# Attention and two MLPs: the first streamed pair's g @ w_out by seven products, first weight slices kept in SBUF, late x, q, k and v in slots

## The chip, the core and the metric

The kernel runs on one core of a Trainium2 chip. The metric is device time in microseconds (us) of one execution. TensorE (PE) multiplies, VectorE (DVE) and ScalarE (ACT) do elementwise work, SyncE (SP) issues the DMA transfers in the order of its queue. Each engine takes its instructions in a fixed order that is settled when the program is built.

## What is computed

Three parts follow each other: a causal linear attention with decay (4 sequences of 768, 8 heads of 64), an MLP with the gate h * sigmoid(1.702 h), and an MLP with the gate max(h, 0) + alpha * min(h, 0). All is fp32.

```python
for t in range(S):
    state = gamma * state + einsum('bhd,bhe->bhde', k[:, :, t], v[:, :, t])
    y[:, :, t] = scale * einsum('bhd,bhde->bhe', q[:, :, t], state)
x = y as 3072 tokens x 512
h = x @ w_in;  g = h * (1 / (1 + exp(-1.702 * h)));  x = g @ w_out      # 512 x 2048, 2048 x 512
h = x @ w_in2; g = maximum(h, 0) + alpha * minimum(h, 0);  out = g @ w_out2
```

## The kernel before

**Precision.** A product of fp32 operands is made of three fp32r matmuls: each operand is split into hi (a rounded copy, made by ACT) and lo (the rest, by a DVE subtraction), and hi*hi, lo*hi and hi*lo are added in PSUM. `g_split`, `x_split`, `piece_hi` and `piece_lo` make such splits. A matmul here has a 128x128 stationary part and 512 moving columns.

**Tokens and blocks.** 24 attention chunks of 128 tokens (`att_scores`, `att_out`, `att_x`, numbered c) make the x of 6 blocks j of 512 tokens. The first MLP's blocks 0 and 1 are multiplied in the plain way, one of 16 slices (ft) of the hidden width at a time: `mlp_h` (12 matmuls) and `mlp_y` (12 matmuls, L558). These are the 32 `steps`. The other work is streamed in five `PAIRS` (layer, pair of blocks): (1,1), (1,2), (2,0), (2,1), (2,2), called 0 to 4 here.

**Pairs by seven products.** A pair's x @ w_in goes through a Strassen-like scheme of 7 products of half blocks in place of 8. For each `quad` (two slices of the hidden width) there are 7 units; `h_unit` (L650) issues 6 matmuls for a unit (L662) and takes one piece of w_in (hi and lo of 256 columns in one slot of 2 KB a partition, `hw`) from DRAM, loaded HRING = 6 units ahead by `load_h`. The pieces are a11, a12, a22 and the combinations s1 to s4, which DVE makes from the raw slices (`conv_sums`, L272, 4 operations for a quad) and `conv_split` (L294) splits and stores to DRAM (`wc`). The pair's g @ w_out runs YLAG = 36 units behind. In pairs 1 to 4 it goes by seven products too (`y_split` L692 makes combinations of g and their splits, `strassen_y` L743 issues 6 matmuls at L760, `y_out` L772 adds the products up). In pair 0 it is plain: `y_chunk` calls `mlp_y` with w_out slices that `load_wo` (L638) brings back from DRAM into a ring of 6 (`woh`, `wol`), 12 matmuls for each of 16 slices and 2 blocks. While it runs, `slice_sums` (L287) adds hi and lo of the same slices up again, from which the combined w_out pieces of pair 1 are made.

**Conversion.** The weights come as 8-byte words and are converted on the chip (`conv_words`, `conv_f32`, L176 to L199), the first layer's beside the plain steps, the second layer's beside pairs 0 and 1 (`W2_AT` gives their slots). In the first layer hi and lo are whole tiles of 512 columns (`whi` L224, `wlo` L242), kept until they are stored and their last plain step is done (`drop`).

**Slots.** Nearly everything in SBUF lives in 82 slots of 2 KB a partition: `take` takes the slot that has been free longest, `give` puts one back; a slot that a store is reading comes back late (`give_stored`, `let_go`). Counting takes and gives through the program, the fewest free slots are 8 at job slot 42, 9 at 76, 4 at 92 and 93, and 4 at 108 and 109.

**Order.** `jobs` is a table by job slot: two job slots for each of the 32 plain steps, so base = 64, then two for 7 units. q, k and v of chunks 4 to 23 and the weights are loaded through `ld`, a ring of 5 tiles, in the order in which the jobs use them (`issue`, L143); the next load is issued when the oldest tile is done. `load_early` (L163) loads chunks 1 to 3 into slots. x of chunks 8 to 15 (pair 0) is written to DRAM by `att_x` (L425) and read back by `x_load`; x of chunks 16 to 23 stays in slots (`att_x_kept`, L434). A scheduler then orders the recorded instructions on each engine, by priority and by when their inputs are there.

Of the kernel before, what the change touches and what calls it, by code (L numbers as in the profile page):

```python
# [8 lines left out]
F32 = mybir.dt.float32  # L9
# [9 lines left out]
P = 128  # L19
# [48 lines left out]
W2_AT = [3 + 1.17 * m for m in range(12)] + [18 + 2 * m for m in range(4)] + [26 + 1.2 * m for m in range(16)]  # L68
# [3 lines left out]
def tile_linear_attention_two_mlps(ctx: ExitStack, tc, qk, kv, w1, w2, consts, alpha, out):  # L72
# [101 lines left out]
    w_hi, w_lo, conv, raw = {}, {}, {}, {}  # L174
# [76 lines left out]
    def put_two(dst, at, part_, src):  # L251
        c = slice(256 * part_, 256 * part_ + 256)
        put(dst[at:at + 2, :, c].rearrange("g p c -> p g c"), src.rearrange("p (g c) -> p g c", g=2))

    def store(key):
        kind, layer, ft = key
        hi, lo = w_hi[key], w_lo[key]
        dst, at = wc[kind, layer, ft // 2], W_AT[kind]
        if kind == "out":
            put(wo[ft][0], hi)  # L260
            put(wo[ft][1], lo)
        elif ft % 2 == 0:
            put_two(dst, at["a11"], 0, hi)
            put_two(dst, at["a11"], 1, lo)
        else:
            put(dst[at["a22"], :, 0:256], hi[:, 256:])
            put(dst[at["a22"], :, 256:512], lo[:, 256:])
        stored.add(key)
# [17 lines left out]

    def slice_sums(i):  # L287
# [4 lines left out]
        conv_sums("out", 1, i)  # L292

    def conv_split(kind, layer, i):  # L294
        for name, s in zip(("s1", "s3"), sums.pop((kind, layer, i))):
# [5 lines left out]
            give_stored(*ws)  # L301
# [101 lines left out]
    def att_x(c):  # L403
        if c >= 4 * BT // C:
            att_x_kept(c)
            return
# [9 lines left out]
        if j < 2:  # L416
            if i == 0:
                new_x(j)
            nc.scalar.copy(out=x_hi[j][:, :, cols], in_=x32)  # L419
            if early_x:  # L420
                att_state(c)
            att[c] = x32
            return
        idx = j // 2 - 1
        for d in range(2):  # L425
            nc.sync.dma_start(
                out=xsd[idx][:, :, d, j % 2, cols].rearrange("k p c -> p k c"), in_=x32[:, 2 * d:2 * d + 2, :]
            )
        att.pop(c)
        give(x32)  # L430
        if c % (2 * BT // C) == 2 * BT // C - 1:
            stored.add(("x", idx))
# [113 lines left out]
    def mlp_y(layer, j, ft, begin, end, carry, w, es=range(NP)):  # L546
        if begin and es[0] == 0:
# [3 lines left out]
        wh, wl = w  # L551
        cols = lambda w, e: w[:, e * P:(e + 1) * P]
        prods = [(e, cols(w, e), gh) for e in es for w in (wh, wl)]
        prods += [(e, cols(wh, e), gl) for e in es]
        seen = [0] * NP
        for e, w, g in prods:
# [490 lines left out]
```

## Time and profile before

| | |
|---|---|
| time, median of 3 runs | 1060.81 us (1060.52 to 1062.38) |
| the profiled execution | 1061.71 us, its span 1059.9 us |
| TensorE busy | 1038.3 us (98%) |
| DVE busy | 849.8 us (80%) |
| ACT busy | 655.2 us (62%) |
| DMA | 292 MB, 276 GB/s over the span |

The span is the time from the first to the last instruction; the execution's own time has some 1.8 us more around it. A busy time is the union of the intervals in which an engine had an instruction at work. The profile also tells which event ended each idle time, the busy time by stretches of the span, and the chain of waits that ended last.

### The profile page before, as it was taken

Reading aid. Unit: us, or ns where it says so; the run is one execution under the profiler, and the core shown is the slowest. Engines: PE = TensorE matmul, PEld = TensorE weight load, DVE = VectorE, ACT = ScalarE, POOL = GpSimd, SP = SyncE. Lnnn points to the kernel's source line nnn. Section 1 sums busy time; section 2 is a strip of 40 time slices with the busy share of each in tenths; the row PEclk is TensorE's granted clock in tenths of the full one; section 3 lists DMA queues with packets and bytes.
Section 4 is the critical chain, followed back from the end, with each engine's and each line's share of the span. In section 5 each row is a group of like instructions: output and inputs, shape, how many; then the busy total and the mean of one; then the engine's idle time right before and its main releaser. Section 6 shows DMA issues by size and latency. Waiting matters only on the chain.

```text
span 1059.9 us, 17734 instructions
## 1 busy us (share of the span) xinstructions
PE 1038.3 (98%) x5980; PEld 848.0 (80%) x5980; DVE 849.8 (80%) x1602; ACT 655.2 (62%) x1344; POOL 0.2 (0%) x4
## 2 busy tenths in 40 slices
PE   8999999999999999999999999999999999999998
PEld 5688887788777888888888878778888888888886
DVE  6999945574568887898899999999786987677792
ACT  7787744454466665556786577777565765556740
POOL 0000000000000000000000000000000000000000
PEclk9999999999999999999999999999999999999999
DMA  8679969789789989999999899888686765675661
GB/s 301 219 257 366 341 232 365 242 290 338 260 304 322 358 299 329 346 332 336 314 306 337 253 323 347 308 275 278 217 270 211 233 221 172 230 253 177 201 199 60
DMA packets 154138, 292.06 MB, mean 276 GB/s; under 512 B 16448, under 2 KB 33216, under 8 KB 154048
## 3 DMA queue, kind: packets, MB, share of 16 engines
q1 hardware_dynamic: 153760, 290.66, 80.8%
q8 instruction: 48, 0.79, 0.3%
q14 instruction: 42, 0.34, 0.1%
q10 hardware_dynamic: 288, 0.27, 0.1%
HBM read 214.32 MB, written 76.55 MB: 274 GB/s over the span
## 4 chain that ended last, share of the span: by engine, by line
PE 78%; DVE 9%; DMA 7%; ACT 3%; issue 2%; SPq 1%; DVEq 0%; ACTq 0%
PE py L760 24%; PE pa L662 16%; PE py L558 16%; PE pd L662 12%; PE ph L537 7%; DMA ld<-kv 2%; DMA wcin<-wb 2%; PE px L361 2%; DVE gl L525 1%; ACT v L326 1%; PE sc L333 1%; DVE gw L517 1%; DMA hw<-wcin 1%; DVE wb L216 1%; DVE gw L677 1%
## 5 line engine op out<-in xcount | busy, mean ns | idle before, releaser
L662 PE MATMUL pa<-xo,hw 128*128 128x512 f32 x960 | 243.6, 390 | 3.8 <-ACT gw L512 2.0
L760 PE MATMUL py<-gh,yw 128*128 128x512 f32 x896 | 240.3, 390 | 1.0 <-DMA yw<-wcout 0.7
L662 PEld LDWEIGHTS pa<-xo,hw 128*128 128x128 f32 x960 | 179.4, 188 | 43.2 <-ACT gw L512 3.0
L760 PEld LDWEIGHTS py<-gh,yw 128*128 128x128 f32 x896 | 167.9, 188 | 37.2 <-DMA yw<-wcout 1.4
L525 DVE TENSOR_TENSOR gl<-gw,gh 128x512 fp32r<-128x512 f32 x224 | 150.2, 688 | 44.6 <-ACT gh L524 38.5
L662 PE MATMUL pd<-xo,hw 128*128 128x512 f32 x720 | 182.7, 390 | 0.0
L524 ACT CAST gh<-gw 128x512 fp32r<-128x512 f32 x224 | 136.2, 620 | 62.6 <-PE py L760 22.5
L662 PEld LDWEIGHTS pd<-xo,hw 128*128 128x128 f32 x720 | 134.8, 188 | 28.3
L760 PE MATMUL py<-gl,yw 128*128 128x512 f32 x448 | 138.3, 390 | 1.8 <-DVE gl L525 1.8
L760 PEld LDWEIGHTS py<-gl,yw 128*128 128x128 f32 x448 | 83.9, 188 | 19.9 <-DVE gl L525 2.6
L517 DVE SCALAR_TENSOR_TENSOR gw<-t,nalpha,gw 128x512 f32<-128x512 f32 x96 | 71.4, 748 | 12.5 <-ACT gw L516 12.3
L515 ACT ACTIVATE t<-gw 128x512 f32<-128x512 f32 x72 | 45.5, 632 | 50.3 <-DVE gw L677 46.3
L773 DVE TENSOR_TENSOR yc<-py,yc 128x512 f32<-128x512 f32 x79 | 50.9, 685 | 26.5 <-PE py L760 26.5
L326 ACT ACTIVATE v<-ld,cst 128x64 f32<-128x64 f32 x168 | 44.4, 336 | 40.1 <-DMA ld<-kv 30.3
L212 ACT CAST wb<-s 128x256 fp32r<-128x256 f32 x128 | 48.0, 404 | 33.6 <-DVE s L279 17.9
L674 ACT COPY gw<-pa 128x512 f32<-128x512 f32 x80 | 46.3, 581 | 25.5 <-PE pa L662 25.1
L677 DVE TENSOR_TENSOR gw<-pd,gw 128x512 f32<-128x512 f32 x80 | 54.9, 686 | 5.0 <-PE pd L662 4.8
L216 DVE TENSOR_TENSOR wb<-s,wb 128x256 fp32r<-128x256 f32 x128 | 50.2, 420 | 8.1 <-ACT wb L212 7.5
L537 PE MATMUL ph<-xhi,whi 128*128 128x512 f32 x128 | 51.4, 402 | 1.5 <-ACT xhi L419 1.1
L558 PE MATMUL py<-gh,whi 128*128 128x512 f32 x128 | 51.2, 400 | 0.5 <-ACT gh L524 0.5
L558 PE MATMUL py<-gh,wlo 128*128 128x512 f32 x128 | 50.1, 392 | 0.0
L537 PE MATMUL ph<-xhi,wlo 128*128 128x512 f32 x128 | 50.1, 391 | 0.0
(100 smaller groups left out, 1608.9 us busy)
## 6 DMA issues: line engine op xcount, KB each, us to landing
hw<-wcin SPq DMA_DIRECT2D x280, 256.0 KB, 4.5
yw<-wcout SPq DMA_DIRECT2D x200, 256.0 KB, 3.6
ld<-w SPq DMA_DIRECT2D x64, 512.0 KB, 5.3
wcin<-wb SPq DMA_DIRECT2D x88, 256.0 KB, 5.0
wcout<-wb SPq DMA_DIRECT2D x88, 256.0 KB, 3.9
ld<-qk SPq DMA_DIRECT2D x21, 512.0 KB, 5.4
ld<-kv SPq DMA_DIRECT2D x21, 512.0 KB, 5.2
xl<-xsd SPq DMA_DIRECT2D x32, 256.0 KB, 4.8
```

The lines of the kernel that those rows point to most:

```text
L212: nc.scalar.copy(out=w[:, 0:256], in_=src)
L216: nc.vector.tensor_tensor(out=w[:, 256:], in0=src, in1=w[:, 0:256].bitcast(F32), op=ALU.subtract)
L326: nc.scalar.activation(out=v[:, h, :], in_=vt[:, h * D:(h + 1) * D], func=AF.Copy, scale=decay_v[:, h:h + 1])
L517: nc.vector.scalar_tensor_tensor(out=g, in0=t, scalar=nalpha[:, ft:ft + 1], in1=g, op0=ALU.mult, op1=ALU.add)
L524: nc.scalar.copy(out=gh, in_=g)
L525: nc.vector.tensor_tensor(out=gl, in0=g, in1=gh.bitcast(F32), op=ALU.subtract)
L537: nc.tensor.matmul(out=ph, lhsT=w[:, k * P:(k + 1) * P], rhs=x[:, k, :], start=(n == 0), stop=(n == len(prods) - 1),)
L558: nc.tensor.matmul(out=py[e], lhsT=w, rhs=g, start=(begin and seen[e] == 1), stop=(end and seen[e] == 3))
L662: nc.tensor.matmul(out=ps, lhsT=w[:, 256 * part_ + k * P:256 * part_ + (k + 1) * P], rhs=x[2 * k + low], start=(n in (0, 1, 3) and m == 0) ...
L677: nc.vector.tensor_tensor(out=g, in0=ps, in1=g, op=ALU.add)
L760: nc.tensor.matmul(out=ps[e], lhsT=w[:, at:at + P], rhs=t, start=(fresh and seen[e] == 1), stop=(m == GQ - 1 and seen[e] == 3), skip_group ...
L773: add_ = lambda o, x: nc.vector.tensor_tensor(out=o, in0=ps, in1=x, op=ALU.add)
```

## The change

Four edits, and what they need:

1. Pair 0's g @ w_out goes by the seven products as in the other pairs (IDX_S, `ysteps`, `load_wo` and the plain branch of `y_chunk` go). So the combined pieces of the first layer's w_out have to be there before pair 0: `slice_sums` and `conv_split` for it become jobs at slots `SUMS_OUT` (47 to 68). For four quads the slices' hi and lo are still in SBUF then; for the other four (`LOADED`) `slice_load` brings them back, two slots earlier. The quads of pair 0 run in the order 6, 7, 4, 5, 0, 1, 2, 3 (`QORD`), those of pair 1 forward.
2. The first layer's weights are split and stored in halves like the second layer's (`stored_parts`, `conv_hi`, `conv_lo`, `store`): one slot holds hi and lo of 256 columns. For quads 6 and 7 (`RESIDENT`) the seven w_in pieces stay in their slots, and the first 14 units take them from there (`resident`, `load_h`, `drop`).
3. x of chunks 8 to 15 stays in slots (`att_x_kept` from chunk 8 on); the write to DRAM and `x_load` of pair 0 go.
4. q, k and v of chunks 16 to 23 are loaded by `load_early` at job slots base + (-5, -3, -1, 1, 2, 3, 4, 5), where their scores stand at base + 0 to 7, instead of through the ring `ld`.

`W2_AT` is changed slightly. The number of slots stays 82; the fewest free ones are now 4 at job slot 42, 3 at 76, 4 at 92 and 93, 6 and 7 at 108 and 109.

```diff
-IDX_S = 1
-QORD = [tuple(range(8)) if i != 1 else tuple(range(7, -1, -1)) for i in range(5)]
-WSTEPS = 6
+QORD = [(6, 7, 4, 5, 0, 1, 2, 3)] + [tuple(range(8))] * 4
+SUMS_OUT = (62, 64, 66, 68, 47, 51, 55, 58)
+LOADED = 4
+RESIDENT = (6, 7)
+LOADS = (-5, -3, -1, 1, 2, 3, 4, 5)
-W2_AT = [3 + 1.17 * m for m in range(12)] + [18 + 2 * m for m in range(4)] + [26 + 1.2 * m for m in range(16)]
+W2_AT = [3 + 1.17 * m for m in range(12)] + [17 + 1.5 * m for m in range(6)] + [26 + 1.25 * m for m in range(14)]
...
     def conv_hi(key):
+        parts = halves(conv[key][0])
+        ms = stored_parts(key) if key[1] == 2 else (0, 1)
+        w_of[key] = {m: piece_hi(parts[m]) for m in ms}
+
+    def conv_lo(key):
+        t = conv.pop(key)[0]
+        for m, w in w_of[key].items():
+            piece_lo(w, halves(t)[m])
...
-        hi = w_hi[key]
-        w_lo[key] = take("wlo", dtype=F32R)
-        nc.vector.tensor_tensor(out=w_lo[key], in0=t, in1=hi.bitcast(F32), op=ALU.subtract)
...
+    def slice_load(i):
+        for f in (2 * i, 2 * i + 1):
+            assert ("out", 1, f) in stored
+            kept[f] = take("wo", dtype=F32R), take("wo", dtype=F32R)
+            for n in range(2):
+                nc.sync.dma_start(out=kept[f][n].bitcast(F32), in_=wo[f][n])
+
     def slice_sums(i):
         for f in (2 * i, 2 * i + 1):
+            ws = kept.pop(f, None)
             raw["out", 1, f] = t = take("wsum")
-            hi, lo = wring[f]
-            nc.vector.tensor_tensor(out=t, in0=hi.bitcast(F32), in1=lo.bitcast(F32), op=ALU.add)
+            for m, part_ in enumerate(halves(t)):
+                hi, lo = halves((ws or w_of["out", 1, f])[m].bitcast(F32))
+                nc.vector.tensor_tensor(out=part_, in0=hi, in1=lo, op=ALU.add)
...
             give(s)
-            give_stored(*ws)
+            if (kind, layer) == ("in", 1) and i in RESIDENT:
+                for m, w in zip(("s1", "s2") if name == "s1" else ("s3", "s4"), ws):
+                    resident[i, m] = w
+            else:
+                give_stored(*ws)
...
     def att_x(c):
-        if c >= 4 * BT // C:
+        if c >= 2 * BT // C:
             att_x_kept(c)
             return
...
             quad, n = units[u]
+            if (quad, W_OF[n]) in resident:
+                hw.append(resident.pop((quad, W_OF[n])))
+                return
             load_piece(hw, "hw", "in", PAIRS[quad // NQ][0], quad % NQ, n)
...
-        if ychunks[c][0] == "o":
-            _, n, half = ychunks[c]
-            idx, t, f = ysteps[n]
...
-            mlp_y(1, 2 * PAIRS[idx][1] + t, f, first, end, None, wring[f], range(2 * half, 2 * half + 2))
...
-        job(s_scores, att_scores, c, load=(("qk", c), ("kv", c)))
+        if c < 4 * per:
+            job(s_scores, att_scores, c, load=(("qk", c), ("kv", c)))
+        else:
+            job(LOADS[c - 4 * per] + base, load_early, c)
+            job(s_scores, att_scores, c)
...
+    for i in range(NQ):
+        if i < LOADED:
+            job(SUMS_OUT[i] - 2, slice_load, i)
+        job(SUMS_OUT[i], slice_sums, i)
+        job(SUMS_OUT[i] + 1, conv_split, "out", 1, i)
```

Three places in the order of the built programs. On TensorE, where pair 0's g @ w_out begins (`pa` is an accumulator of a unit, `py` one of g @ w_out, `gh` and `gl` the split g), before:

```order
L662 MATMUL pa<-xo,hw 128x512 x6
L558 MATMUL py_4108<-gh,woh 128x512
L558 MATMUL py_4108<-gh,wol 128x512
L558 MATMUL py_4109<-gh,woh 128x512
L558 MATMUL py_4109<-gh,wol 128x512
L558 MATMUL py_4108<-gl,woh 128x512
L558 MATMUL py_4109<-gl,woh 128x512
L662 MATMUL pa<-xo,hw 128x512 x6
```

and now:

```order
L632 MATMUL pa<-xo,hw 128x512 x12
L632 MATMUL pd<-xo,hw 128x512 x12
L632 MATMUL pa<-xo,hw 128x512 x6
L705 MATMUL py<-gh,yw 128x512 x4
L705 MATMUL py<-gl,yw 128x512 x2
L632 MATMUL pa<-xo,hw 128x512 x6
L705 MATMUL py<-gh,yw 128x512 x4
L705 MATMUL py<-gl,yw 128x512 x2
```

The chunks stand at the same place behind the units, six matmuls each; before there were 64 such chunks in the pair, now 56.

On the DMA queue (SP), beside units 9 to 21, where the late chunks' q, k and v are loaded (`ld` is the ring, `early` a slot, `w` second-layer words, `wcout` the store of combined w_out pieces), before:

```order
L610 DMA hw<-wcin_3_91 128x512
L610 DMA hw<-wcin_2_90 128x512
L151 DMA ld<-w 128x1024
L151 DMA ld<-qk 128x1024
L151 DMA ld<-kv 128x1024
L151 DMA ld<-w 128x1024
L610 DMA hw<-wcin_3_91 128x512
```

and now:

```order
L171 DMA early<-qk 128x512 x2
L171 DMA early<-kv 128x512 x2
L238 DMA wcout_2_106<-wb 128x512 x4
L591 DMA hw<-wcin_4_92 128x512
L591 DMA hw<-wcin_5_93 128x512
L591 DMA hw<-wcin_4_92 128x512
L591 DMA hw<-wcin_5_93 128x512
L171 DMA early<-qk 128x512 x2
L171 DMA early<-kv 128x512 x2
L153 DMA ld<-w 128x1024
```

The loads of q, k and v are out of the ring, and stores of combined w_out pieces stand between them.

On DVE, beside units 37 to 43 of pair 0, with the first chunks of g @ w_out (`cvt` is a weight in conversion, `t` and `gw` on L668 combinations of g), before:

```order
L677 TENSOR_TENSOR gw<-pa,gw 128x512
L525 TENSOR_TENSOR gl<-gw,gh 128x512
L188 TENSOR_SCALAR cvt<-cvt 128x512
L191 TENSOR_SCALAR cvt<-cvt 128x512
L194 ISA cvt<-cvt,cvr 128x1024
L677 TENSOR_TENSOR gw<-pa,gw 128x512
L525 TENSOR_TENSOR gl<-gw,gh 128x512
L195 SCALAR_TENSOR_TENSOR cvt<-ld,cvt 128x512
```

and now:

```order
L190 TENSOR_SCALAR cvt<-cvt 128x512
L193 TENSOR_SCALAR cvt<-cvt 128x512
L196 ISA cvt<-cvt,cvr 128x1024
L668 TENSOR_TENSOR t_4586<-gw 128x512
L197 SCALAR_TENSOR_TENSOR cvt<-ld,cvt 128x512
L668 TENSOR_TENSOR t_4542<-gw 128x512
L668 TENSOR_TENSOR gw<-gw,t_4586 128x512
L668 TENSOR_TENSOR gw<-gw,t_4542 128x512
L514 TENSOR_TENSOR gl<-t_4542,gh 128x512
L514 TENSOR_TENSOR gl<-t_4619,gh 128x512
```

The differences of `y_split` (L668) now stand here too, between the conversion's operations and the splits.

## Rows read from the trace of the kernel before

**Rows 1.** The page: busy us (share of the span) and instructions by engine.

```profile
PE 1038.3 (98%) x5980; PEld 848.0 (80%) x5980; DVE 849.8 (80%) x1602; ACT 655.2 (62%) x1344; POOL 0.2 (0%) x4
```

**Rows 2.** Stretches: from:to, length, busy us by engine (instructions), clock, DMA share, GB/s.

```profile
60.00:140.00 80.00, 80.00 (x384) 66.07 (x378) 71.93 (x140) 59.25 (x115) 0.00 (x0) 1.00 0.94 328
140.00:246.20 106.20, 104.05 (x945) 83.41 (x944) 65.71 (x143) 49.87 (x130) 0.00 (x0) 1.00 0.85 292
246.20:326.40 80.20, 76.50 (x815) 61.93 (x814) 49.30 (x118) 44.37 (x117) 0.00 (x0) 1.00 0.81 287
326.40:489.80 163.40, 162.43 (x715) 133.82 (x714) 135.50 (x280) 96.95 (x203) 0.00 (x0) 1.00 0.96 338
489.80:560.00 70.20, 70.20 (x311) 58.12 (x311) 64.34 (x123) 53.66 (x107) 0.00 (x0) 1.00 0.93 314
560.00:720.00 160.00, 156.26 (x683) 127.21 (x682) 156.02 (x293) 115.46 (x226) 0.00 (x0) 1.00 0.91 308
720.00:1005.60 285.60, 285.60 (x1262) 236.57 (x1261) 223.67 (x353) 177.21 (x312) 0.00 (x0) 1.00 0.70 222
```

**Rows 3.** Timeline of PE at 740 us: start, us, engine, line, operation, count.

```profile
740.27 1.52 PE L662 MATMUL pa<-xo,hw 128*128 128x512 f32 x6
741.63 1.07 PE L760 MATMUL py<-gh,yw 128*128 128x512 f32 x4
742.99 1.52 PE L662 MATMUL pa<-xo,hw 128*128 128x512 f32 x6
```

**Rows 4.** Groups by line and shape: pair 0's plain matmuls, first and last of three.

```profile
L558 PE MATMUL py<-gh,woh 128*128 128x512 f32 x128 | 49.8, 389 | 0.0
...
L558 PE MATMUL py<-gl,woh 128*128 128x512 f32 x128 | 39.4, 389 | 0.0
```

**Rows 5.** Timeline of DVE at 666 us, operations that follow each other without a gap.

```profile
666.13 0.68 DVE L525 TENSOR_TENSOR gl<-gw,gh 128x512 fp32r<-128x512 f32 x1
666.73 0.42 DVE L216 TENSOR_TENSOR wb<-s,wb 128x256 fp32r<-128x256 f32 x1
667.07 0.42 DVE L216 TENSOR_TENSOR wb<-cvt,wb 128x256 fp32r<-128x256 f32 x1
```

**Rows 6.** Groups on DVE: count, busy us and mean ns, idle us before them.

```profile
L242 DVE TENSOR_TENSOR wlo<-cvt,whi 128x512 fp32r<-128x512 f32 x32 | 21.9, 685 | 0.7 <-ACT whi L224 0.7
...
L216 DVE TENSOR_TENSOR wb<-cvt,wb 128x256 fp32r<-128x256 f32 x48 | 19.6, 420 | 2.6 <-ACT wb L212 2.6
...
L291 DVE TENSOR_TENSOR wsum<-woh,wol 128x512 f32<-128x512 f32 x16 | 10.5, 685 | 2.7 <-PE py L558 2.7
...
L442 DVE TENSOR_TENSOR xl<-px,cst 128x128 f32<-128x128 f32 x16 | 4.4, 282 | 0.7 <-PE pu L361 0.7
```

**Rows 7.** Waits of ACT and PE, 246.2 to 326.4 us: us in total, times, longest.

```profile
ACT v L326 <- DMA ld<-kv: 23.2, 6, 5.7
...
PE pa L662 <- ACT gw L512: 2.0, 2, 1.1
```

**Rows 8.** The chain of waits: start, us, what.

```profile
167.18 6.22 DMA wcin<-wb
...
304.16 6.33 DMA ld<-kv
```

**Rows 9.** Waits of PE from 560 to 720 us, the longest.

```profile
PE py L760 <- DVE gl L525: 1.8, 1, 1.8
```

**Rows 10.** DMA: a load to landing; the queue's wait for DVE; the fullest 20 us.

```profile
ld<-kv SPq DMA_DIRECT2D x21, 512.0 KB, 5.2
...
SPq L249 <- DVE wb L216: 56.3, 40, 5.3
...
340.00:360.00 20.00, 20.00 (x89) 16.23 (x88) 16.02 (x31) 13.46 (x27) 0.00 (x0) 1.00 1.05 398
```

More of the change, by code (lines that the diff above doesn't have):

```diff
@@ L255, in store @@
     def store(key):
         kind, layer, ft = key
[L257 to L267, printed above, removed]
+        first = {("in", 0): "a11", ("in", 1): "a22", ("out", 0): "a11", ("out", 1): "a12"}[kind, ft % 2]
@@ L268, in store @@
+        for n, m in enumerate(stored_parts(key)):
+            if (kind, layer) == ("out", 1):
+                dst = wo[ft][m]
+            else:
+                dst = wc[kind, layer, ft // 2][W_AT[kind][first] + n]
+            put(dst, w_of[key][m])
         stored.add(key)
@@ L415, in att_x @@
         cols = slice(i * C, (i + 1) * C)
[L416 to L432, printed above, removed]
+        if i == 0:
+            new_x(j)
+        nc.scalar.copy(out=x_hi[j][:, :, cols], in_=x32)
+        if early_x:
+            att_state(c)
+        att[c] = x32
     def att_x_kept(c):
         banks = att.pop(c)
-        t, i = divmod(c - 4 * BT // C, BT // C)
+        t, i = divmod(c % (2 * BT // C), BT // C)
         for k in range(2):
@@ L544, in mlp_h, with mlp_y @@
             g_of[1, j, ft] = g_split(g)
-    def mlp_y(layer, j, ft, begin, end, carry, w, es=range(NP)):
-        if begin and es[0] == 0:
+    def mlp_y(layer, j, ft, begin, end, carry, w):
+        if begin:
             for e in range(NP):
@@ L550, in mlp_y @@
         gh, gl = g_of[layer, j, ft]
[L551 to L554, printed above, removed]
+        prods = [(e, cols(w, low, e), gh) for e in range(NP) for low in range(2)]
+        prods += [(e, cols(w, 0, e), gl) for e in range(NP)]
         seen = [0] * NP
-        for e, w, g in prods:
+        for e, lhsT, g in prods:
             seen[e] += 1
             nc.tensor.matmul(
-                out=py[e], lhsT=w, rhs=g, start=(begin and seen[e] == 1), stop=(end and seen[e] == 3)
+                out=py[e], lhsT=lhsT, rhs=g, start=(begin and seen[e] == 1), stop=(end and seen[e] == 3)
             )
@@ L926, in drop @@
             if key in stored:
-                give(w_hi.pop(key), w_lo.pop(key))
+                kind, _, ft = key
+                keep = {}
+                if kind == "in" and ft // 2 in RESIDENT:
+                    keep = {m: {0: ("a11", "a12"), 1: ("", "a22")}[ft % 2][m] for m in stored_parts(key)}
+                for m, w in w_of.pop(key).items():
+                    if m in keep:
+                        resident[ft // 2, keep[m]] = w
+                    else:
+                        give(w)
             else:
@@ L931, in finish_step @@
     def finish_step(s, step):
-        w = w_hi["out", 1, step[2]], w_lo["out", 1, step[2]]
-        mlp_y(*step, w)
+        mlp_y(*step, w_of["out", 1, step[2]])
         if uses["out", step[2]] == s:
@@ L947, in tile_linear_attention_two_mlps @@
         let_go(2)
-        if s == NF + LEAD:
-            for u in range(HRING):
-                load_h(u)
-    load_wo(0)
     for s, step in queue:
@@ L954, in tile_linear_attention_two_mlps @@
     drop()
+    for u in range(HRING):
+        load_h(u)
     turn = {"split": 0, "chunk": 0}
@@ L964, in y_turn @@
             turn["chunk"] += 1
-    old = 4 * NF * IDX_S
     for u in range(len(units)):
@@ L969, in tile_linear_attention_two_mlps @@
         past = u + 1 - YLAG
+        if past == -2 * YRING:
+            for c in range(YRING):
+                load_y(c)
         if past > 0:
-            y_turn(min(8 * past // NU, old) + max(0, past - old * NU // 8))
+            y_turn(past)
         if u % NU in (3, 6):
```

133 lines of the change are left out of this document (40 added, 93 removed).

## The prediction, made before the result was known

> **What bounds the kernel now.** I read the page's busy times first: TensorE is busy 1038.3 us of the span of 1059.9, DVE 849.8, ACT 655.2 [rows 1]. 21.6 us are left in which TensorE does nothing, so a change pays here only if it takes matmuls away or takes some of those 21.6 us, and it costs as soon as it adds idle time. Then the stretches [rows 2]; I name them by what runs in them. B (140 to 246.2 us) is the rest of the first two blocks with attention chunks 8 to 15, C (246.2 to 326.4) the first 36 units of g = gate(x @ w_in) with chunks 16 to 23, D (326.4 to 489.8) the first streamed pair's g @ w_out beside units, E (to 560) and F (to 720) the next pair with the second layer's weight conversion, G the rest. The idle time of TensorE (length less busy) is 2.15 in B, 3.70 in C, 0.97 in D, 0 in E, 3.74 in F and 0 in G. DVE is at 92% in E, where TensorE never waits, and at 97.5% in F, where it waits; the wait seen there is one for gl by DVE, 1.8 us [rows 9]. The granted clock is 1.00 in every stretch, the upper level of 2.4 GHz. In the timeline twelve matmuls of 128x512 follow each other in 742.99 - 740.27 = 2.72 us [rows 3]: 0.2267 us each is the price of a matmul on the path.
>
> The profiled execution took 1061.7 us, the median of the runs is 1060.8: I sum against 1061.7 and take 0.9 off at the end.
>
> **TensorE.** In D the old form is three groups of 128 matmuls, 384 in all [rows 4]. The new form has 2 groups of quarters x 7 products x 4 slice pairs x 6 matmuls = 336. 48 fewer, 48 x 0.2267 = 10.9 us, all on the path, since D is TensorE's by 162.43 of 163.40 us. Everything else on TensorE has the same count. The Trainium skill, page "TensorE: Matmul & The Clock Gate", section "Wait — 56ns, not 53.3ns?", gives 215.7 ns from start to start for 512 columns at the upper clock. By that the saving would be 10.4 us; the rows of this kernel say 226.7 ns, and I use them.
>
> **DVE.** Back to back, an operation on 512 columns takes 666.73 - 666.13 = 0.60 us and one on 256 takes 667.07 - 666.73 = 0.34 [rows 5]; the line through both gives an estimate of 0.21 for 128. The change adds:
> - hi and lo of the first layer's weights in halves: 64 x 0.34 for 32 x 0.60 (L242 goes, L216 grows) [rows 6], +2.6 us, nearly all before 140 us.
> - sums of the w_out slices in halves: 32 x 0.34 for 16 x 0.60 (L291) [rows 6], +1.3.
> - x of chunks 8 to 15 written by 32 operations of 128 columns for 16 of 256 (the form is L442) [rows 6]: 6.7 - 5.4 = +1.3, in B.
> - the pair's seven products: 24 more splits, 32 differences, and 20 additions for 4 copies: (24 + 32 + 16) x 0.60 = +43.2 in D.
> Together +48 us. And it moves: the 16 + 32 + 32 operations that make the combined w_out pieces leave D (9.6 + 10.9 + 10.9 = 31.4 us) and go to B and C. Counted in the order between the matmuls that begin and end the stretches, DVE's work grows by 1.8 before B, 22.6 in B, 14.8 in C, 15.7 in D (11.8 by the above, the rest is second-layer conversion that comes earlier) and falls by 7.2 behind D. B then has 65.7 + 22.6 = 88 busy of 106, C 49.3 + 14.8 = 64 of 80: room in both. D has 135.5 + 15.7 = 151 of 163.4 - 10.9 = 152.5, that is 99%. So in D the cover is gone, and the nearest row is F, not E. At F's rate (3.74 idle in 160 us) D would have 3.6 us of idle time, 2.6 more than now; at E's rate 1.0 less; with two waits like F's 1.8 on top, about 6 more. I take **+2.6**, bounds -1.0 and +6. F itself gets shorter at its end, since the conversion is done 7 us of DVE work earlier: **-0.5**, bounds -2 and 0. Before B, DVE is full as well, but TensorE is unbroken from 60 us on: **+0.5**, bounds 0 and +2.6. ACT grows by about 23 us over the run (some 10 in D, to 107 of 152) and has room everywhere.
>
> **Loads and the SP queue.** In C, ACT waits 23.2 us for kv of the late chunks, in six pieces, while TensorE waits 2.0 for a gate by the same ACT [rows 7]; the chain of waits goes through such a load at 304 us [rows 8]. The loads come late because they pass through the ring of five tiles, which the weights of the second layer share, and each waits for an older tile to be done. After the change they go to slots, two to five turns of the job list ahead (two turns are 7 units, 7 x 80.2 / 36 = 15.6 us, against 5.2 us from issue to landing [rows 10]). That takes ACT's wait away, and with it at best all of C's 3.7. Against it: bytes issued in C, counted from the order, grow from 23.9 to 28.0 MB, or 349 GB/s over 80.2 us where 287 ran; D sustains 338 at 96% of the DMA engines [rows 2], and one stretch of 20 us 398 [rows 10]. At 338, C would be 82.8 us long, +2.6; at 398 nothing. I take **-1.5**, bounds -3.7 and +2.6. The Trainium skill, page "DMA: Bandwidth & Descriptors", section "Where 436 GB/s comes from", puts a core's limit between HBM and SBUF at about 358 GB/s. By that C would need 28.0 / 0.358 = 78.2 us, just inside; the 398 of the row exceeds it, so the row decides. In B the round trip of x through DRAM goes (2.1 MB out, 2.1 in) and the fourteen w_in pieces that stay cost no load; nothing there was waited for, so nothing is booked.
>
> **Slots.** The stretch at 167 us shows what a short list of free slots does: a store is still reading a slot that ACT wants, 6.2 us [rows 8]. Counted from the program, four are free there instead of eight, and around slots 75 to 77 (early D) three instead of nine; at 108 and 109 (F) six instead of four. The first I book at **0**, bounds -1.7 and +2; the second is in D's upper bound, the third in F's lower one.
>
> **Sum.** -10.9 + 2.6 - 0.5 + 0.5 - 1.5 + 0 = -9.8. 1061.7 - 9.8 = 1051.9 for a profiled execution, and 0.9 less, 1051.0, for the median.
>
> **Rivals.**
> 1. DVE and the short slot list in D take back half: D at its upper bound (+6), no gain in C: -10.9 + 6 + 0.5 - 0.5 = -4.9, 1055.9. For it: 99% by the count, and y_split's differences stand in front of the splits that TensorE waits for, on one in-order queue. Against it: E at 92% shows no wait at all, and busy times overlap by some 0.08 us for each operation (0.68 long, 0.60 apart [rows 5]), so 99% busy is nearer 93% in steps.
> 2. The idle time goes with the work: C's 3.7, D's 1.0, F's 2.0 and the 1.7 of the wait at 167 us all disappear: -19, 1042; half of that beside the matmuls gives 1046.
> 3. The gain is eaten exactly (within 0.2%): D at +6, C at +2.6 and B at +2. Each would have to come out at its bound.
> 4. Slower. The late chunks' loads stand behind stores of combined w_out pieces on SP, and a store there waits for DVE's lo half, up to 5.3 us at a time [rows 10]. A chunk starts to wait once its load is issued 15.6 - 5.2 = 10.4 us behind its place; beyond that, each us is paid up to eight times, once a chunk. It decides from 13 / 8 = 1.6 us, that is from 12 us of lateness on; at 13 us C loses 8 x 2.6 = 21 and the run takes 1071. For it: DVE is fuller in C and stores come in fours. Against it: two of the stores' longest waits would have to add up, DVE is at 80% in C, and 23.2 us of such waiting of ACT now cost TensorE no more than 3.7.
>
> **How the numbers follow.** The forecast's own case (1048.5 to 1054) has 0.55, rival 1 (1054 to 1058.7) 0.20, rival 2 (below 1048.5) 0.15, rival 3 0.05, rival 4 0.05. A measurement of this kernel can tell about 0.2%, 2.1 us, from no change. The range 1046 to 1058 keeps the forecast's case, nearly all of rival 1 and the upper half of rival 2. Faster by over 0.2%: 0.90; within: 0.05; slower: 0.05.
>
> **What will show it.** TensorE with 48 matmuls fewer and D some 9 us shorter; the step still 0.2267 and the clock 1.00. DVE busy about 900 in all, near 98% in D, with waits of TensorE for gl there of 2 to 4 us; none or few would speak for E's rate. ACT's wait for late kv gone, C at 78 to 80 us. F's idle time at 3 or less. I am wrong if TensorE waits over 5 us in D, or in C for loads, or if the first block (before 140 us) gets longer by more than 1 us.

## The result and the profile after

The kernel after takes 1045.44 us (median of 4 runs, 1043.22 to 1046.52), the kernel before beside it 1061.60: a ratio of 0.9845, 95% interval 0.9827 to 0.9864. Two later comparisons on other chips gave 0.9846 (0.9822 to 0.9870) and 0.9841 (0.9820 to 0.9862). That is 16.2 to 17.5 us less. The forecast of 1051.0 had the right sign and the right largest term, but the time lies below its range of 1046 to 1058.

The page of after, the row that answers to [rows 1]:

```profile
PE 1024.5 (98%) x5932; PEld 838.9 (81%) x5932; DVE 890.1 (85%) x1738; ACT 671.8 (65%) x1404; POOL 0.2 (0%) x4
```

TensorE has 5980 - 5932 = 48 matmuls fewer, DVE 40 us more work. Of the span of 1041.4 us TensorE is idle for 16.9, where it was 21.6. Below are the stretches of after, B to F, with the columns of [rows 2], cut at nearly the same units as those of before (C and D part one unit, 6 matmuls, earlier here, and F ends some ten matmuls later; the table further down goes by units exactly):

```profile
140.00:246.40 106.40, 104.03 (x945) 83.21 (x942) 85.51 (x218) 55.02 (x149) 0.00 (x0) 1.00 0.78 272
246.40:322.00 75.60, 74.40 (x810) 60.53 (x809) 66.94 (x167) 51.22 (x137) 0.00 (x0) 1.00 1.00 373
322.00:474.30 152.30, 152.30 (x673) 126.16 (x672) 146.00 (x283) 105.41 (x210) 0.00 (x0) 1.00 0.91 325
474.30:544.50 70.20, 70.20 (x311) 58.16 (x310) 62.41 (x116) 51.68 (x101) 0.00 (x0) 1.00 0.95 332
544.50:704.00 159.50, 157.67 (x693) 129.38 (x692) 156.31 (x290) 114.02 (x223) 0.00 (x0) 1.00 0.93 315
```

D (third row) is the place to look. DVE is busy 146.0 of 152.3 us, 96%, and TensorE is busy for every one of the 152.3: 672 matmuls x 0.2267. TensorE's timeline has the pace of [rows 3], six matmuls of a unit and six of a chunk in 743.67 - 740.95 = 2.72 us:

```profile
740.95 1.52 PE L632 MATMUL pd<-xo,hw 128*128 128x512 f32 x6
...
743.67 0.61 PE L632 MATMUL pa<-xo,hw 128*128 128x512 f32 x2
```

At the fullest of D the operations of DVE follow each other without a gap, in steps of 0.60 us as in [rows 5]:

```profile
343.19 0.69 DVE L514 TENSOR_TENSOR gl<-t,gh 128x512 fp32r<-128x512 f32 x1
343.79 0.69 DVE L668 TENSOR_TENSOR gw<-gw,t 128x512 f32<-128x512 f32 x1
```

The Trainium skill, "TensorE: Matmul & The Clock Gate", section "Wait — 56ns, not 53.3ns?", has 215.7 ns from start to start for 512 columns at the upper clock; D of this kernel gives 152.3 / 672 = 226.7 ns, and the measurement decides.

In C the waits that answer to [rows 7], of after:

```profile
PE pa L632 <- DMA hw<-wcin: 0.7, 1, 0.7
...
ACT gw L501 <- DVE gw L647: 12.3, 8, 3.6
```

ACT's 23.2 us for late kv are gone; ACT now waits for DVE, and TensorE once for a w_in piece. The wait for gl of [rows 9] has no counterpart; in F the longest is now for a gate by ACT, 0.9 us. C's DMA moves 373 GB/s over 75.6 us at a busy share of 1.00. The Trainium skill, "DMA: Bandwidth & Descriptors", section "Where 436 GB/s comes from", puts a core's limit between HBM and SBUF at about 358 GB/s, the half of a stack's 716 GB/s; here one core is at work and this stretch is above that, so the limit is not a bound here.

**Traces repeat less well than times.** So both kernels were profiled again. The table gives lengths from the first matmul of one unit to that of another: C is unit 0 to 36, D 36 to 92, E 92 to 112, F 112 to 204 (longer than F of the prediction). Unbroken, D takes 720 x 0.2267 = 163.2 us with the old form and 152.3 with the new, E 54.4, F 250.2. What a stretch takes over that is called its excess. It is more than TensorE's idle time: D of before has an excess of 1.6 us and 0.97 us of idle time, F of after 2.8 and 1.8.

| run | to unit 0 | C | D | E | F | rest |
|---|---|---|---|---|---|---|
| before | 246.0 | 79.0 | 164.8 | 54.4 | 255.9 | 259.8 |
| b2_before | 246.3 | 76.9 | 165.4 | 54.9 | 255.4 | 259.8 |
| after | 246.4 | 75.6 | 152.3 | 54.4 | 253.0 | 259.7 |
| a2_after | 245.0 | 76.2 | 152.3 | 54.4 | 254.0 | 259.7 |
| a3_after | 246.4 | 75.4 | 152.3 | 54.4 | 252.3 | 259.7 |
| e1_ring | 246.5 | 78.5 | 158.4 | 54.4 | 253.6 | 259.7 |
| e2_before_slots | 245.2 | 76.2 | 163.3 | 54.4 | 260.2 | 259.8 |
| e3_w2_old | 246.5 | 75.8 | 152.3 | 54.4 | 262.1 | 259.7 |
| e4_before_w2 | 244.8 | 75.7 | 165.5 | 54.4 | 253.0 | 259.8 |
| e12_before_slots_w2 | 246.9 | 78.5 | 163.4 | 54.4 | 253.2 | 259.8 |
| e9_dveD28 | 245.1 | 76.6 | 154.0 | 56.4 | 253.2 | 259.7 |
| e10_dveEF28 | 244.1 | 75.3 | 152.3 | 54.4 | 268.2 | 259.7 |
| e13_83_w2d | 247.6 | 74.3 | 152.3 | 54.4 | 250.9 | 260.1 |

From the mean of the two traces of before to the mean of the three of after: up to unit 0 -0.3, C -2.2, D -12.8, E -0.3, F -2.5, rest -0.1, in all -18.2 us. The profiled executions of after are among its shorter ones; in which stretch the others lose their 1 to 3 us no trace shows.

### The profile page after: what moved, and what is told of

The parts are those of the page before. It is cut to its first block, busy times and chain, and to the rows that moved or that the text cites. A ratio compares the mean times of both kernels' runs of the same rounds, so it can differ in the third digit from the quotient of the medians.

```text
span 1041.4 us, 17905 instructions
## 1 busy us (share of the span) xinstructions
PE 1024.5 (98%) x5932; PEld 838.9 (81%) x5932; DVE 890.1 (85%) x1738; ACT 671.8 (65%) x1404; POOL 0.2 (0%) x4
## 4 chain that ended last, share of the span: by engine, by line
PE 86%; DVE 7%; DMA 4%; ACT 1%; SPq 1%; issue 1%; DVEq 0%; ACTq 0%
PE py L705 36%; PE pa L632 20%; PE pd L632 15%; PE ph L530 6%; PE py L549 6%; PE px L361 2%; PE sc L333 1%; DMA hw<-wcin 1%; DVE wb L218 1%; DMA wo<-wo 1%; DVE s L260 1%; DVE a L344 1%; DMA ld<-kv 1%; DVE xo L458 1%; DMA early<-qk 1%
## 5 line engine op out<-in xcount | busy, mean ns | idle before, releaser
L705 PE MATMUL py<-gh,yw 128*128 128x512 f32 x1120 | 299.7, 389 | 0.9 <-ACT gw L644 0.7
L705 PEld LDWEIGHTS py<-gh,yw 128*128 128x128 f32 x1120 | 210.1, 188 | 45.2 <-ACT gw L644 1.1
L705 PE MATMUL py<-gl,yw 128*128 128x512 f32 x560 | 172.7, 389 | 0.0
L705 PEld LDWEIGHTS py<-gl,yw 128*128 128x128 f32 x560 | 105.0, 188 | 22.1 <-DVE gl L514 0.4
L719 DVE TENSOR_TENSOR yc<-py,yc 128x512 f32<-128x512 f32 x99 | 63.7, 683 | 25.5 <-PE py L705 25.4
L530 PE MATMUL ph<-xhi,wb 128*128 128x512 f32 x256 | 65.4, 396 | 1.3 <-ACT xhi L418 1.1
L549 PE MATMUL py<-gh,wb 128*128 128x512 f32 x256 | 65.5, 396 | 0.1
L530 PEld LDWEIGHTS ph<-xhi,wb 128*128 128x128 f32 x256 | 47.0, 188 | 12.0 <-ACT xhi L418 1.3
L549 PEld LDWEIGHTS py<-gh,wb 128*128 128x128 f32 x256 | 47.1, 188 | 11.6 <-ACT gh L513 0.6
L183 ACT ACTIVATE cvt<-ld 128x512 f32<-128x512 f32 x64 | 43.1, 673 | 17.2 <-DMA ld<-w 12.0
```

The source lines that it names most:

```text
L530: nc.tensor.matmul(out=ph, lhsT=cols(w, low, k), rhs=x[:, k, :], start=(n == 0), stop=(n == len(prods) - 1),)
L549: nc.tensor.matmul(out=py[e], lhsT=lhsT, rhs=g, start=(begin and seen[e] == 1), stop=(end and seen[e] == 3))
L705: nc.tensor.matmul(out=ps[e], lhsT=w[:, at:at + P], rhs=t, start=(fresh and seen[e] == 1), stop=(m == GQ - 1 and seen[e] == 3), skip_group ...
L719: add_ = lambda o, x: nc.vector.tensor_tensor(out=o, in0=ps, in1=x, op=ALU.add)
```

## The experiments

The 48 matmuls need no experiment: D's rows show them. The question is the other 5 to 7 us, which the forecast put at +1.1. The theory: edit 4 (late q, k and v out of the ring) takes away idle time in C and D, and the new W2_AT takes it in F; DVE at 96% in D costs nothing. The rivals: the gain is that of the resident w_in pieces, or of the free slots, or one execution's luck. Where a run had no run of after beside it, after is taken as 0.9844 (the mean of the three ratios) of before on the same chip.

**Both kernels again.** The kernels are unchanged.

> The kernel before once more, on the chip of the experiments. Theory (stretch C's length of 79.0 us belongs to the kernel before: late loads in the ring): C is again 78.5 to 79.5 us, with a wait of ACT for late kv of 20 us or more. Rival (C varies from one execution to the next with the landing of the same loads in the same order): C is near 75.6 us, and then most of the 3.4 us forecast from one trace is not the change's.

> The kernel after once more, on the chip of the experiments. Theory (the gain over before is the matmuls' 10.9 us, and the rest depends on the execution): ratio to before about 0.987 to 0.990, D unbroken at 152.3 us, F's idle time between 1.5 and 4 us. Rival (all 16 us are the change's): ratio 0.9845 again, F's idle time 1.8 us.

b2_before 1060.88 us (ratio 1.0006, 0.9991 to 1.0022), a2_after 1043.77 (ratio 0.9846). So the 16 us are the change's, against the first theory of a2_after; D was unbroken again, and F's excess 3.8 us in place of 2.8 (its idle time 2.5 in place of 1.8). C of before was 76.9 and not 79.0. ACT's wait in C of b2_before:

```profile
ACT v L326 <- DMA ld<-kv: 21.3, 7, 5.1
```

and in C of e4_before_w2 (below), whose order is the same up to there:

```profile
ACT v L326 <- DMA ld<-kv: 16.4, 6, 5.5
```

21.3 us of ACT's waiting went with a C of 76.9, 16.4 with 75.7, 23.2 with 79.0. C of one trace is good to some 3 us, and with the ring it is 77.2 in the mean of the three. Neither expectation for C holds: it is not 79 each time, and the mean is above after's 75.7 by 1.5 us.

**Edit 4 undone in after, and done alone in before.** e1_ring:

```diff
-        if c < 4 * per:
-            job(s_scores, att_scores, c, load=(("qk", c), ("kv", c)))
-        else:
-            job(LOADS[c - 4 * per] + base, load_early, c)
-            job(s_scores, att_scores, c)
+        job(s_scores, att_scores, c, load=(("qk", c), ("kv", c)))
```

e2_before_slots is the reverse in the kernel before.

> The kernel after with edit 4 undone: q, k and v of chunks 16 to 23 go through the ring ld again. Theory (the ring's late loads made stretch C's idle time): ACT's wait for late kv returns at about 20 us, C (first unit to unit 36) goes from 75.6 back to about 79 us, all else stays: +3.4 us, about 1048.9. Rival (C's gain came from the 14 units that take w_in from SBUF): C stays within 0.7 us of 75.6 and the time within 1 us of the kernel after.

> The kernel before with edit 4 alone: q, k and v of chunks 16 to 23 by slots. Theory of the ring: ACT's wait of 23.2 us for kv goes, C falls from 79.0 to about 75.6 us, -3.4 us, about 1057.4. Rival (without the resident w_in pieces the loads of C do not fit, or the gain is theirs): C falls by less than 0.7 us; with loads that do not fit it grows, at 338 GB/s by up to 2.6.

e1_ring 1051.34 us, ratio 0.9928 (0.9905 to 0.9952): 8.9 us more than after, against 3.4 expected. Its nine runs spread from 1046.69 to 1057.93, and the trace is of one that took 1053.01. There C has 2.8 of it, near what was expected, though ACT's wait for late kv is 11.6 us and not 20; but D has 6.1. The longest wait of the SP queue in e1_ring, 318 to 334 us:

```profile
SPq L153 <- DVE cvt L197: 4.3, 1, 4.3
```

The queue's timeline there (start, us, engine, line, transfer, count):

```profile
318.12 4.98 SPq L153 DMA_DIRECT2D ld<-w  x2
323.16 3.35 SPq L238 DMA_DIRECT2D wcin<-wb  x5
326.61 0.60 SPq L153 DMA_DIRECT2D ld<-w  x1
327.25 1.62 SPq L591 DMA_DIRECT2D hw<-wcin  x3
```

TensorE's timeline behind it, with the idle time ahead of a row in brackets:

```profile
333.65 2.90 PE L632 MATMUL pd<-xo,hw 128*128 128x512 f32 x6 [2.86 <-DMA hw<-wcin]
336.34 1.91 PE L705 MATMUL py<-gh,yw 128*128 128x512 f32 x4
```

And two stretches of 4 us, columns as in [rows 2]:

```profile
334.00:338.00 4.00, 4.00 (x10) 3.12 (x10) 3.67 (x8) 1.58 (x3) 0.00 (x0) 0.50 1.04 410
338.00:342.00 4.00, 4.00 (x16) 3.21 (x15) 2.39 (x5) 0.06 (x1) 0.00 (x0) 0.80 1.05 398
```

A load into the ring waits 4.3 us for DVE to be done with the ring's oldest tile, and the SP queue, which goes in order, holds the w_in loads back behind it and behind five stores. TensorE waits 2.86 us for one, and then runs at a granted clock of 0.50, the level of 1.2 GHz, with 10 matmuls in 4 us in place of 18: D's 6.1 us are some 3 us more than the wait.

e2_before_slots 1058.61, ratio 0.9996 (0.9979 to 1.0013). In its trace D's excess fell from 1.6 and 2.2 us to 0.1, and its idle time to nothing, which is half of the answer: before, TensorE's wait in D was not for DVE's work but for slots and queues. The chain of waits of before at 326 us:

```profile
322.77 5.11 DMA wcin<-wb
...
327.96 0.41 ACT wb L212
328.36 0.49 ACT gw L674
328.86 0.04 issue
328.90 0.50 PE pa L662
```

ACT waited for a slot that a store was reading, and the copy that empties an accumulator for TensorE (the third row) stood behind that. But F of e2_before_slots is 4.6 us longer than before, so nothing was left in the time. (A part of that is the clock: a wait of 2.1 us at 670 us is followed by 0.61 from 672 to 676 us, with 10 matmuls in those 4 us.) That the loads in slots end such waits in D the traces show both ways; by which steps they do it only e1 shows.

**W2_AT.** e3_w2_old puts the old W2_AT into after, e4_before_w2 the new one into before, e12_before_slots_w2 adds edit 4 to that:

```diff
-W2_AT = [3 + 1.17 * m for m in range(12)] + [17 + 1.5 * m for m in range(6)] + [26 + 1.25 * m for m in range(14)]
+W2_AT = [3 + 1.17 * m for m in range(12)] + [18 + 2 * m for m in range(4)] + [26 + 1.2 * m for m in range(16)]
```

> The kernel after with the old W2_AT (slots of the second layer's weight conversion). Theory (F's gain is the conversion that comes earlier): idle time of TensorE in F goes from 1.8 back to 3.7 us or more, time +2 to +2.8, about 1048. Rival (F's gain comes from elsewhere, the slot list or the order of the loads): within 0.7 us of the kernel after.

> The kernel before with the new W2_AT alone. Theory (conversion earlier): F's idle time falls from 3.7 to about 1.8 us, D's grows by at most 0.5 since DVE has 28 us of room there, time -1.5 to -2.8, about 1059. Rival: F within 0.7 us of before, or, with four free slots at the units concerned, +0.5 to +2 us.

> The kernel before with edit 4 and the new W2_AT together. Theory (beside the 48 matmuls the whole gain is these two): C about 76, D about 163.4 (unbroken is 163.2), F's idle time 2 to 3 us, 5 to 6 us less than before, about 1054.5. Rival (each alone gave 0.4 and 2.5, they only add): 3 us less. Third (edit 4 makes F worse, as it did alone): no gain.

e3_w2_old 1051.95, ratio 0.9936 (0.9918 to 0.9954), 9.5 us more than after where 2 to 2.8 were expected, 9.0 of it in F (262.1 for 253.1). e4_before_w2 1056.45, ratio 0.9980 (0.9966 to 0.9993), 2.5 us less than before, F 253.0. e12_before_slots_w2 1055.52, ratio 0.9958 (0.9943 to 0.9973), 5.0 us less than before: with the matmuls' 10.9 that is 15.9 of the 16.2 to 17.5. If the parts add up, the rest of the change, stores in halves, x in slots and the resident pieces, is worth what is left, 0 to 2 us; e12's interval alone is 3 us wide. (The profiled execution of e12 was its longest, 1057.91; in its C TensorE waited 2.1 us for a w_in piece, and the clock fell behind that too.)

The costliest wait of e3, 4.0 us before 607.47, in the chain of waits:

```profile
603.62 0.34 DVE cvt L193
603.96 0.60 DVE gl L514
604.56 0.60 DVE gw L647
605.16 0.66 DVE gw L506
605.82 0.60 DVE cvt L196
606.42 0.35 DVE wb L218
606.77 0.04 issue
606.81 0.61 ACT gh L513
607.42 0.04 issue
607.47 1.65 PE py L705 x3
```

It is DVE back to back, with the conversion's operations (`cvt`, `wb`) between those of gate and split. Of the conversions 11 begin in F with the old table (26 + 1.2 m from 32 on, where F begins) and 9 with the new.

**More DVE work.** Operations of 512 columns are added whose results are not used; first with inputs that are there from the start, e6_dve12 and e7_dve28:

```diff
...
+            if idx == 0 and c % 5 == 0:  # e7_dve28: c % 2
+                nc.vector.tensor_tensor(out=more, in0=cst[:, 0:512], in1=cst[:, 0:512], op=ALU.add)
```

> The kernel after with 12 more DVE operations of 512 columns in D, one beside every fifth chunk of pair 0's g @ w_out (their results are not used): 12 x 0.60 = 7.2 us of DVE work in a stretch of 152.3 us in which DVE is busy for 146.0. Theory (busy times overlap; by steps of 0.60 and 0.34 us D's DVE work is 141 us, so 148.5 still fits): D stays unbroken, within 0.5 us of 152.3, the time within 1 us of the kernel after. Rival (at the rate of F, 98% busy, TensorE waits): D +2 to +4 us.

> As the one with 12, with 28 more DVE operations in D, one beside every second chunk of pair 0's g @ w_out: 28 x 0.60 = 16.8 us. Theory (by steps 141 + 17 = 158 us of DVE work in 152.3): DVE becomes the bound in D, D +4 to +6 us or, if the work runs on beside E, where DVE has 8 us left, +1 to +3; a single wait over 3 us would cost 4 more by the clock that falls behind it. Rival (DVE has more room than the steps say): D within 0.5 us.

1046.92 and 1048.93 us, 3.2 and 5.2 above after, with D unbroken in both. This tells nothing of D: the scheduler had put the operations where their inputs were there, as the trace of e7 shows.

```profile
L667 DVE TENSOR_TENSOR more<-cst x28: 679/686/695, 10.0 to 159.6; 128x512 f32<-128x512 f32 x28
```

What it does give is the price of the first block: 7.2 us of DVE work there cost 3.2 (its interval overlaps that of after, but unit 0 begins at 250.6 in its trace, some 4.7 us late), 16.8 cost 5.2. Then with the chunk's own gh as input, beside pair 0's chunks (D), and beside pair 1's (E and the first half of F):

```diff
...
+    def extra(c):
+        if ychunks[c][0] == 0 and c % 2 == 0:  # e10_dveEF28: == 1
+            with tc.high_priority(HG):
+                nc.vector.tensor_tensor(out=more, in0=ysplit[c][0].bitcast(F32), in1=cst[:, 0:512], op=ALU.add)
```

> The kernel after with 28 more DVE operations of 512 columns, one behind the split of every second chunk of pair 0's g @ w_out; each reads the gh of its chunk, so it can't run earlier than D (the results are not used). 28 x 0.60 = 16.8 us on top of 141 us of steps in 152.3 us. Theory (a full DVE costs nothing until its steps exceed the stretch): 158 in 152.3, so D or the first units behind it grow by 1 to 6 us. Rival of the forecast (at 98% busy TensorE waits as it does in F): by 6 us or more, with waits over 3 us and the clock falling behind them. Third (the splits run far enough ahead): 0.

> The same 28 operations beside pair 1's g @ w_out instead (E and the first half of F, 474 to 626 us, DVE busy 19 of 20 us, no wait of TensorE now). Theory (in F the gate of the second layer has a DVE operation between a unit and its split, so the same load costs more there than in D): 3 us or more above what D's 28 operations cost. Rival (a full DVE costs the same wherever it is): the same cost as in D within 2 us.

e9_dveD28 1048.46 (ratio 0.9905, 0.9877 to 0.9933), 4.9 above after by the medians (its four runs go from 1046.78 to 1053.16); e10_dveEF28 1059.84 (0.9995, 0.9978 to 1.0012), 16.3 above. In the trace of e9, 26 of the 28 operations begin in D, and D is 1.7 us longer. E is 2.0 longer too, most of it by a wait of 1.6 us at 519 us behind a load of x that landed at 517; that the added work made this load late is not shown. In the trace of e10, 3 of the 28 begin in D and 8 in E, and both stay unbroken; the other 17, 10.2 us of DVE work, begin in F, and F is 15.1 us longer. Stretches of e9 at the fullest of D:

```profile
340.00:360.00 20.00, 20.00 (x90) 16.55 (x89) 20.00 (x38) 15.87 (x34) 0.00 (x0) 1.00 0.64 223
360.00:380.00 20.00, 20.00 (x90) 16.55 (x89) 20.00 (x38) 15.46 (x32) 0.00 (x0) 1.00 0.94 321
380.00:400.00 20.00, 19.35 (x83) 15.05 (x82) 19.32 (x38) 14.02 (x27) 0.00 (x0) 1.00 0.95 327
```

and of e10 in F:

```profile
580.00:600.00 20.00, 15.13 (x62) 10.83 (x62) 18.63 (x38) 10.50 (x21) 0.00 (x0) 1.00 0.72 234
660.00:680.00 20.00, 17.09 (x72) 12.82 (x71) 19.86 (x39) 12.27 (x26) 0.00 (x0) 1.00 0.91 299
```

The second row lies behind the last added operation, which begins at 628 us. TensorE is idle there for 2.9 us, after from 660 to 680 us for 0.2: by work that was put off, or by waits that F has in some executions anyway; the trace doesn't tell. With DVE at 20.0 of 20 us for 40 us TensorE is unbroken in D; with 18.6 of 20 it loses 4.9 us in F. TensorE's largest sum of waits in F of e10 is for w_in pieces:

```profile
PE pa L633 <- DMA hw<-wcin: 5.8, 4, 3.4
```

and the waits of its SP queue from 560 to 600 us:

```profile
SPq L592 <- PE py L711: 5.9, 5, 1.9
SPq L592 <- DVE cvt L197: 4.3, 3, 2.6
SPq L239 <- DVE wb L219: 4.2, 4, 1.8
SPq L592 <- DVE gl L515: 4.2, 2, 3.3
```

L239 are stores of converted pieces, L592 the loads of w_in and w_out pieces. The loads wait most for TensorE itself, 5.9 us, which is late by then, and next for a DVE that is behind (for their slot), the stores for DVE too; TensorE then waits for a weight, not for g. Whether this or the longer gate of the second layer makes most of F's price, these runs don't separate.

**Slots and resident pieces.** e5_slots80 has `NSLOT = 80`; e8_no_resident has `RESIDENT = ()` and issues the first six loads at the end of the last plain step (the kernel before does so ten steps earlier; the expectation says that wrongly):

```diff
-RESIDENT = (6, 7)
+RESIDENT = ()
...
+        if s == NF + LEAD + 10:
+            for u in range(HRING):
+                load_h(u)
```

> The kernel after with 80 slots for 82: two fewer free ones everywhere (1 at job slot 76 for 3, 2 at 42 for 4). Theory (the short slot list costs little, since D is unbroken): within 1.5 us of the kernel after, D within 0.5 us of 152.3. Rival (slots still read by a store are what ends the remaining waits in B, C and F): +3 us or more, with waits of ACT and DVE for stores.

> The kernel after without the pieces that stay in SBUF (all of pair 0's w_in pieces come from DRAM, the first six loaded where the kernel before loads them). Theory (nothing waited for these loads before, the edit only gives the DMA room): C within 1 us, the time within 1.5 us of the kernel after. Rival (with x, q, k and v and the stores the loads of C don't fit: it moves 373 GB/s now with 14 pieces or 3.7 MB fewer): C grows by 3.7 MB / 373 GB/s = 10 us at worst, 3 us or more.

e5_slots80 1045.88 (0.9866, 0.9851 to 0.9881), 2.3 above after, D unbroken: a small price at most, for its interval overlaps those of after. e8_no_resident 1061.28 (1.0014, 0.9996 to 1.0031), 17.7 above, far beyond either expectation, but by another mechanism than bandwidth. The timeline of its SP queue before the first unit:

```profile
251.43 3.68 SPq L238 DMA_DIRECT2D wcin<-wb  x4
255.43 2.83 SPq L238 DMA_DIRECT2D wcout<-wb  x4
258.51 6.51 SPq L591 DMA_DIRECT2D hw<-wcin  x10
```

Quads 6 and 7, the last that are converted, come first in the new order. From DRAM their loads stand behind their own stores, until 258.5 us, and unit 0 begins at 264.1 in place of 245.9. With all pieces from DRAM this order of quads costs what the change gains. From unit 0 to the end e8 takes 793.5 us, after 795.0: the whole loss lies before unit 0.

**Better tables and one more slot.** e11_w2h, e11_w2i and e11_w2d change the last twenty entries of W2_AT, e13_83_w2d has `NSLOT = 83` and the table of e11_w2d:

```diff
-W2_AT = ... + [17 + 1.5 * m for m in range(6)] + [26 + 1.25 * m for m in range(14)]
+W2_AT = ... + [17 + 1.2 * m for m in range(20)]                                      # e11_w2h; e11_w2i: 1.1
+W2_AT = ... + [17 + 1.5 * m for m in range(6)] + [26 + 1.4 * m for m in range(14)]   # e11_w2d, e13_83_w2d
```

> The kernel after with the last twenty conversions of the second layer at 17 + 1.2 m instead of 17 + 1.5 m (6) and 26 + 1.25 m (14): two of nine leave F for D. Theory (DVE work costs several times more in F than in D): F's idle time under 1 us, D within 1 us of 152.3, the time 0.5 to 2 us below the kernel after, about 1043. Rival (D is at its limit): D +1 to +3, no gain or slower.

> The same with 17 + 1.1 m: three of nine leave F for D. Theory: F unbroken but for what is not the conversion's, D +0 to +2, the time 0 to 2 us below the kernel after. Rival (D is at its limit): D +2 to +5, slower by 1 to 4.

> The kernel after with the last fourteen conversions at 26 + 1.4 m instead of 26 + 1.25 m: nine stay in F, but the last ends two job slots (7 units, 15 us) later. Theory (what costs in F is how much DVE work is left there): within 1 us of the kernel after. Rival (what costs is its density): F's idle time falls by 1 us or more.

> The kernel after with 83 slots for 82 and the last fourteen conversions at 26 + 1.4 m. Theory (80 slots cost 2.1 us, so one more gives about 1; the thinner conversion gives 0 to 1): 0 to 2 us below the kernel after. Rival (the waits left have other causes, the chain of the second layer's gate and the first block): the same within 1 us.

> The kernel after on the same chip, to compare with: ratio to before 0.983 to 0.987, D unbroken at 152.3 us.

e11_w2h 1048.03 (0.9886, 0.9871 to 0.9901), 4.0 above after; e11_w2i 1045.38 (0.9867, 0.9848 to 0.9885), 1.4 above; e11_w2d 1043.95 (0.9852, 0.9836 to 0.9868), the same as after. D stayed unbroken in all three: in e11_w2h and e11_w2i it takes two and three more conversions for nothing. But E got 4.7 and 1.5 us longer in these two, and F (254.4, 253.3 and 253.4 us) didn't get shorter than the 253.1 of after. The waits moved forward; the theory that fewer conversions in F are enough falls. e13_83_w2d took 1041.07 (1040.67 to 1041.92), a3_after beside it 1043.54 (1042.18 to 1044.39): 2.5 us less, a little more than expected; the two sets of runs don't overlap. Its D and F:

```profile
321.80:474.10 152.30, 152.30 (x673) 126.16 (x672) 143.69 (x279) 104.81 (x208) 0.00 (x0) 1.00 0.92 325
528.60:779.40 250.80, 250.38 (x1105) 207.09 (x1104) 231.43 (x415) 171.32 (x323) 0.00 (x0) 1.00 0.88 293
```

F is idle for 0.4 us only. One slot more with the thinner table does there what the table alone didn't, in one trace of each.

## Why the prediction missed

| term | forecast | bounds | traces, mean of 2 and of 3 |
|---|---|---|---|
| 48 matmuls | -10.9 | | -10.9 |
| D, idle time (traces: excess) | +2.6 | -1.0 to +6 | -1.9 |
| C | -1.5 | -3.7 to +2.6 | -2.2 |
| F (and E) | -0.5 | -2 to 0 | -2.8 |
| up to unit 0 | +0.5 | 0 to +2.6 | -0.3 |
| sum | -9.8 | | -18.1 |

**The matmuls** are right to 0.1 us: 163.2 to 152.3 unbroken.

**D is the step that failed**: "the nearest row is F, not E". It put 3.6 us of idle time into D, 2.6 more than before, and three executions of after have none: off by 3.6 us in the trace that the sum was made on (0.97 to 0), by 4.5 in the table. The count behind it nearly held (151 us of DVE work forecast, 146.0 measured; over the run 900, and 890.1), but the busy share of DVE is not what makes TensorE wait in D. Shown by e9: 16.8 us more, 26 of 28 operations in D, cost 1.7 there. The prediction had the argument for it under its first rival (operations overlap by 0.08 us, so 99% busy is nearer 93% in steps) and gave it no weight in the sum. And the idle time that D had before came from slots and a queue, not from a full DVE: with edit 4 D's excess is 0.1 (e2, e12), without it 1.6 to 6.1. So D's lower bound, -1.0, is what came in the trace of before; the wait behind that idle time is in its chain of waits at 322.77 to 328.90, at D's beginning, and the prediction made no use of it.

**F** was mis-sized, -0.5 where -2.5 came (-1.9 by idle time in the first traces). I booked the new W2_AT as an earlier end of the conversion. That the table makes this gain is shown: e4 gave -2.5 us by itself, e3 +9.5. By what steps is not: two conversions fewer begin in F, where e10's DVE work cost most, but two and three fewer again (e11_w2h, e11_w2i) brought nothing. I called the table's change slight, and took it by its size.

**C** came out near its term. Against the trace that the sum was made on it is -3.4, against three executions in the old order -1.5. The bytes (349 GB/s) were no limit.

**Before unit 0** the DVE work added cost nothing that shows. By e6 and e7 it would have cost a third to a half of its length, had it all come before 160 us. The short slot list, booked at 0, is not told apart: two slots fewer everywhere cost 2.3 us (e5), within the noise.

Of the rivals the second was nearest, in which the idle time goes with the work; its half-way point was 1046. It had D's and F's idle time right (1.0 and 1.9 us less); C kept 1.2 of its 3.7 us, and the idle time of B stayed (2.4 us for 2.2). It gave no reason, and got 0.15; that the time lies next to its half-way point is in part luck. The fourth, loads held up behind stores on SP, did not happen in after. It happened in e8; in e1 a load into the ring blocked the queue, and stores behind it.

Open: why edit 4 alone, with the old table, makes F longer by 4.6 us (e2) is not explained; one trace of it shows stores that hold slots as well as DVE back to back. Open too is why DVE work costs so much more in F than in D.

## What to carry to other kernels

A busy share alone doesn't tell what an engine's next microsecond costs: some 16 us of DVE work cost 1.7 us in one stretch (D, DVE at 96%), and 10 us cost 15 in another (F, at 98%), and only adding work in place, with inputs that keep it there, told them apart. Read what an idle time waits for, through the queue, before putting it down to the engine that is full: here a ring shared by two kinds of loads, and slots that stores still held. Sum against several traces, not one: a stretch of 79 us came out at 76.9 and 75.7 in the same order.

## What the runs showed of the hardware

The granted clock of TensorE can make a wait twice as dear. In e1 a wait of 2.86 us was followed by 4 us at 0.50 (10 matmuls in 334 to 338 us), in e3 one of 3.98 by a like stretch (8 matmuls in 607 to 611 us):

```profile
607.00:611.00 4.00, 3.53 (x8) 2.81 (x9) 4.00 (x9) 3.08 (x7) 0.00 (x0) 0.50 0.83 259
```

The length of the wait does not decide it alone. In e12 a wait of 2.1 us was followed by a fall, in e11_w2h one of 1.78 at 612 us too; the 1.8 us of the kernel before at 674 us were not, and in e10 not even the 3.4 us up to 584.27, against what the expectation of e7_dve28 says of waits over 3 us:

```profile
584.00:588.00 4.00, 3.73 (x16) 2.98 (x17) 3.33 (x8) 3.04 (x6) 0.00 (x0) 1.00 0.77 290
```

The stretches of [rows 2] have 1.00 throughout, so no number of the prediction allowed for it.
